# An attention and feed-forward kernel whose opening is reordered: batch 0 in overlapped halves, v used where it was loaded, batch 1 ahead of the output weights, one output tile held back

## The chip, the cores and the metric

The kernel runs on one core of a Trainium2 chip. The metric is device time in microseconds, from launch to end of one execution. A core has five engines that run side by side, each with its own instruction stream in order: PE (TensorE, matmuls), DVE (VectorE), ACT (ScalarE), POOL (GpSimd) and SP (SyncE, here only a DMA queue). They meet through semaphores. SBUF is the on-chip memory, PSUM the small memory into which PE writes its sums.

## What is computed

Eight batches of eight heads, 576 positions, head size 64: linear attention with an RMS norm, then a feed-forward layer over all 4608 tokens.

```python
kv = np.einsum('bhsd,bhse->bhde', k, v)
out = np.einsum('bhsd,bhde->bhse', q, kv)
rms = np.sqrt(np.mean(out * out, axis=-1, keepdims=True) + 1e-06)
attn = out / rms * g_norm
x = attn.transpose(0, 2, 1, 3).reshape(B * S, H * D)      # 4608 x 512
h = x @ w_in                                              # 512 x 2048
g = np.maximum(h, 0.0) + alpha * np.minimum(h, 0.0)
y = g @ w_out                                             # 2048 x 512
```

All inputs and the output are float32. The kernel computes in float16 with float32 sums.

## The kernel before, in words

The 4608 tokens are cut into nine windows of 512 tokens; a window does not end where a batch of 576 ends. Heads are taken in four pairs j, so that a pair fills 128 partitions.

**Loading.** All loads are issued from POOL, in program order, and are cast to float16 on the way. The first 512 positions of a batch go to a staging tile (`kst`, `vst`, `qst`, two of each), whose partition p holds positions 4p to 4p+3 of every head; the last 64 positions, the remainder, go straight to the fifth slot of the batch's tile (`ksb`, `vsb`, `qsb`, three of each). Regrouping (`regroup`, L133) copies staging to the batch's tile, so that the two heads of a pair lie side by side.

**Attention of a pair.** `step_t` transposes q by five matmuls of 128 columns and evacuates on DVE (qt). `step_kv` sums k times v over five matmuls; DVE masks the result (kv). `step_ot` multiplies them into a tile of 512 tokens (ot), which ACT squares. `step_ssq` sums the squares by a matmul with a block mask; ACT takes Ln and Exp (`rstd`), and DVE writes the normalised tile `xt`. qt and kv share one PSUM buffer (`ps_s`), ot has two, ssq has one.

**Feed-forward.** For window w and each of 16 groups g of 128 hidden units: four w_in matmuls (`m1_mm`) into one of three `h` buffers, evacuated by ACT (`m_sb`) and DVE (`gt`). Then a tile a of 128 tokens gets 16 w_out matmuls (`y_mm`), one for each g; ACT copies it (`y_out`) and SP stores it.

**Order.** The program is recorded in the order in which it is written, engine by engine. Opening: batch 0 in two halves of four heads, one after the other; ten matmuls on constants at the start, and a few between (`keep_warm`), only keep PE busy. First pass over w_in: 16 groups of window 0. First pass over w_out: the four tiles ya, yb, yc, yd of window 0 at once (three of them in the h buffers), g outermost, with window 1's attention steps put in from g = 6. Loop of window 1: its w_in groups, with window 2's attention from g = 4. From window 2 on a loop holds w_in of w, w_out of w - 1 and attention of w + 1. The last window's w_out follows alone.

**Queues around the change.** POOL issues batch 0, the four quarters of w_in, then batch 1 and w_out mixed, then batches 2 and 3. Regrouping stands on DVE (and for v of batch 0 on ACT) up to batch 2, on POOL from batch 3 on.

## Time and profile before

| | |
|---|---|
| median of three runs | 329.71 us (329.23 to 330.53) |
| profiled execution | 329.75 us, span 328.0 us |
| PE busy | 298.4 us, 91% |
| ACT, DVE, POOL busy | 53%, 49%, 23% |
| mean granted clock of PE | 0.99 |
| w_in matmul of 512 columns, mean | 384 ns x576 |
| w_out matmul of 512 columns, mean | 379 ns x512 |

The means are longer than the pace, since matmuls follow each other before the one ahead has left the array. A row of the timeline gives start, duration and, in brackets, how long the engine stood idle before it and what ended that. A row of waits gives who waited for whom, the sum, the number and the longest. In the table of stages the three numbers at the end are granted clock, mean number of busy DMA slots per engine and GB/s.

### The profile page before, as it was taken

Reading aid. Unit: us, or ns where it says so; the run is one execution under the profiler, and the core shown is the slowest. Engines: PE = TensorE matmul, PEld = TensorE weight load, DVE = VectorE, ACT = ScalarE, POOL = GpSimd, SP = SyncE. Lnnn points to the kernel's source line nnn. Section 1 sums busy time; section 2 is a strip of 40 time slices with the busy share of each in tenths; the row PEclk is TensorE's granted clock in tenths of the full one; section 3 lists DMA queues with packets and bytes.
Section 4 is the critical chain, followed back from the end, with each engine's and each line's share of the span. In section 5 each row is a group of like instructions: output and inputs, shape, how many; then the busy total and the mean of one; then the engine's idle time right before and its main releaser. Section 6 shows DMA issues by size and latency. Waiting matters only on the chain.

```text
span 328.0 us, 4205 instructions
## 1 busy us (share of the span) xinstructions
PE 298.4 (91%) x1593; PEld 143.7 (44%) x1593; DVE 160.2 (49%) x271; ACT 173.4 (53%) x291; POOL 74.7 (23%) x80
## 2 busy tenths in 40 slices
...
GB/s 95 193 203 202 198 195 191 223 145 83 38 178 33 34 126 154 34 33 149 134 32 34 32 32 34 51 13 53 36 23 21 59 38 34 32 32 34 44 86 64
DMA packets 47621, 28.07 MB, mean 86 GB/s; under 512 B 14304, under 2 KB 42992, under 8 KB 47600
## 3 DMA queue, kind: packets, MB, share of 16 engines
...
## 4 chain that ended last, share of the span: by engine, by line
PE 83%; ACT 7%; DVE 4%; DMA 2%; issue 1%; POOL 1%; POOLq 0%; ACTq 0%
PE h_ps L300 36%; PE y_ps L322 34%; PE kv_ps L237 3%; PE ssq_ps L268 2%; PE qt_ps L222 2%; PE ot_ps L256 2%; ACT rstd L270 2%; DMA qsb<-in_q_dram 2%; ACT rstd L273 2%; DVE xt L275 1%; DVE gt L309 1%; ACT sq_sb L262 1%; ACT m_sb L307 1%; PE yd L322 1%; DVE qt_sb L231 1%
## 5 line engine op out<-in xcount | busy, mean ns | idle before, releaser
L300 PE MATMUL h_ps<-xt,w_in_sb 128*128 128x512 f16 x576 | 147.3, 384 | 4.1 <-ACT y_sb L329 1.5
L309 DVE SCALAR_TENSOR_TENSOR gt<-m_sb,beta_sb,h_ps 128x512 f16<-128x512 f32 x144 | 106.8, 745 | 88.4 <-ACT m_sb L307 86.9
L307 ACT ACTIVATE m_sb<-h_ps 128x512 f32<-128x512 f32 x144 | 85.1, 593 | 83.7 <-PE h_ps L300 83.6
L322 PE MATMUL y_ps<-w_out_sb,gt 128*128 128x512 f16 x512 | 128.8, 379 | 0.0
L322 PEld LDWEIGHTS <-gt 128*128 128x128 f16 x576 | 56.0, 98 | 67.5 <-issue 2.3
L300 PEld LDWEIGHTS <-w_in_sb 128*128 128x128 f16 x576 | 54.9, 99 | 67.2 <-issue 14.5
L275 DVE SCALAR_TENSOR_TENSOR xt<-ot_ps,g2col,rstd 128x512 f16<-128x512 f32 x36 | 27.0, 751 | 46.5 <-ACT rstd L273 46.5
L270 ACT ACTIVATE rstd<-ssq_ps,eps_t 128x512 f32<-128x512 f32 x36 | 24.7, 686 | 18.2 <-PE ssq_ps L268 18.2
L262 ACT ACTIVATE sq_sb<-ot_ps 128x512 f16<-128x512 f32 x36 | 21.3, 597 | 22.6 <-PE ot_ps L256 22.1
L329 ACT COPY y_sb<-y_ps 128x512 f32<-128x512 f32 x32 | 18.7, 585 | 18.4 <-PE y_ps L322 18.4
L273 ACT ACTIVATE rstd<-rstd 128x512 f32<-128x512 f32 x36 | 22.7, 629 | 1.1
L268 PE MATMUL ssq_ps<-sq_sb,mask 128*128 128x512 f16 x36 | 13.6, 378 | 7.0 <-ACT sq_sb L262 5.5
L222 PE MATMUL qt_ps<-ident,qsb 128*128 128x128 f16 x160 | 14.8, 227 | 5.7 <-DVE qsb L139 4.8
L237 PE MATMUL kv_ps<-vsb,ksb 128*128 128x128 f16 x160 | 14.5, 226 | 4.7 <-DVE qt_sb L231 4.7
L222 PEld LDWEIGHTS <-qsb 128*128 128x128 f16 x160 | 11.8, 101 | 13.5 <-DVE qsb L139 5.9
L231 DVE COPY qt_sb<-qt_ps 128x576 f16<-128x576 f16 x32 | 14.3, 451 | 6.4 <-PE qt_ps L222 6.3
L237 PEld LDWEIGHTS <-ksb 128*128 128x128 f16 x160 | 11.9, 101 | 12.1 <-issue 6.1
L256 PE MATMUL ot_ps<-qt_sb,kv_sb 128*128 128x512 f16 (+7 forms) x64 | 14.2, 296 | 0.3 <-DVE kv_sb L245 0.3
L128 POOL DMA_DIRECT2D ksb<-in_k_dram x8 | 5.6, 700 | 36.4 <-PE kv_ps L237 27.8
L139 POOL COPY ksb<-kst 128x2048 f16<-128x2048 f16 x5 | 9.5, 1893 | 18.7 <-DMA kst<-in_k_dram 18.7
L139 POOL COPY qsb<-qst 128x2048 f16<-128x2048 f16 x5 | 9.5, 1894 | 7.4 <-DMA qst<-in_q_dram 7.4
L139 POOL COPY vsb<-vst 128x2048 f16<-128x2048 f16 x5 | 9.5, 1894 | 6.8 <-DMA vst<-in_v_dram 6.8
...
## 6 DMA issues: line engine op xcount, KB each, us to landing
...
```

What stands on the lines that cost most here:

```text
L139: (eng or nc.vector).tensor_copy(out=dst, in_=src)
L222: nc.tensor.matmul(out=qt_ps[:, t * P : (t + 1) * P], lhsT=qs[:, t, 2 * j : 2 * j + 2, :], rhs=ident16[:], is_transpose=True, start=(t == ...
L237: nc.tensor.matmul(out=kv_ps[:], lhsT=ks[:, t, 2 * j : 2 * j + 2, :], rhs=vs[:, t, 2 * j : 2 * j + 2, :], start=(t == 0), stop=(t == NT - 1),)
L256: nc.tensor.matmul(out=ot_ps[:, n0 - w * W : n1 - w * W], lhsT=kvs[b, j][:], rhs=qts[b, j][:, n0 - b * S : n1 - b * S], start=True, stop=True,
L262: nc.scalar.activation(out=sq[:], in_=ot_ps[:], func=AF.Square)
L270: nc.scalar.activation(out=rstd[:], in_=ssq_ps[:], func=AF.Ln, bias=eps_t[:], scale=inv_d,)
L273: nc.scalar.activation(out=rstd[:], in_=rstd[:], func=AF.Exp, bias=0.0, scale=-0.5)
L275: nc.vector.scalar_tensor_tensor(out=xts[w, j][:], in0=ot_ps[:], scalar=g2col[:], in1=rstd[:], op0=ALU.mult, op1=ALU.mult,)
L300: nc.tensor.matmul(out=h_ps[:], lhsT=w_in_blk(c, g), rhs=xts[w, c][:], start=(c == 0), stop=(c == NC - 1),)
L307: nc.scalar.activation(out=m_sb[:], in_=h_ps[:], func=AF.Relu, scale=-1.0)
L309: nc.vector.scalar_tensor_tensor(out=gt[:], in0=m_sb[:], scalar=beta_sb[:, g : g + 1], in1=h_ps[:], op0=ALU.mult, op1=ALU.add,)
L322: nc.tensor.matmul(out=y[:], lhsT=gts[w, g][:, a * P : (a + 1) * P], rhs=w_out_blk(g), start=(g == 0), stop=(g == NF - 1),)
```

## The change

- The remainder of batch 0 is loaded by SP as float32 into three output buffers; ACT casts it into place.
- v is no longer regrouped. `step_kv` reads its four main slices from the staging tile as two runs of 64 columns that lie 256 elements apart, and the fifth from the small `vsb` tile.
- POOL loads batch 0 as q, k, v of heads 0 to 3, then of heads 4 to 7; k and q of batch 1 come ahead of the first quarter of w_out, v of batch 1 right behind it.
- In the opening the transposes and kv products of the second half stand before the end of the first half's normalisation (`ssq_mm` and `norm` are now apart).
- Batch 1's k and q are regrouped on DVE inside the first pass over w_in, batch 2's on POOL.
- The first pass over w_out makes three tiles, with window 1's attention spread from g = 0 to g = 12; the fourth tile's 16 matmuls go into window 1's loop, one for each g.

```diff
@@ -94,6 +94,12 @@
     warm16 = const_p.tile([P, W], FP16, name="warm16")
     nc.vector.memset(warm16[:], 0.5)
 
+    rem0 = {}
+    for nm, src in (("q", q), ("k", k), ("v", v)):
+        rem0[nm] = ysb_p.tile([P, H, D], FP32, name=f"rem0{nm}", tag="y_sb")
+        nc.sync.dma_start(
+            out=rem0[nm][0:REM], in_=src[0, :, MAIN:S, :].rearrange("h s d -> s h d"),
+        )
     alpha_row = const_p.tile([NF, P], FP32, name="alpha_row")
     nc.sync.dma_start(out=alpha_row[:], in_=moe_alpha[:].rearrange("(g p) -> g p", p=P))
     g2col = const_p.tile([P, 1], FP32, name="g2col")
@@ -109,8 +115,9 @@
     for i in range(NBUF):
         t = {}
         for nm in ("k", "v", "q"):
-            t[nm] = qkv_p.tile([P, NT, H, D], FP16, name=f"{nm}sb{i}")
-            nc.vector.memset(t[nm][REM:P, TPP, :, :], 0.0)
+            n = 1 if nm == "v" else NT
+            t[nm] = qkv_p.tile([P, n, H, D], FP16, name=f"{nm}sb{i}")
+            nc.vector.memset(t[nm][REM:P, n - 1, :, :], 0.0)
         bufs.append(t)
     stages = {}
 
@@ -126,7 +133,7 @@
 
     def load_rem(b, nm):
         nc.gpsimd.dma_start(
-            out=bufs[b % NBUF][nm][0:REM, TPP, :, :],
+            out=bufs[b % NBUF][nm][0:REM, 0 if nm == "v" else TPP, :, :],
             in_=srcs[nm][b, :, MAIN:S, :].rearrange("h s d -> s h d"),
         )
 
@@ -144,7 +151,7 @@
             load_main(b, nm, 0, H)
 
     def regroup_batch(b):
-        for nm in ("k", "v", "q"):
+        for nm in ("k", "q"):
             regroup(b, nm, 0, H, nc.gpsimd)
 
 
@@ -178,25 +185,21 @@
         i, r = divmod(g, GW)
         return w_out_sb[i][:, r, :]
 
-    for nm in ("k", "v", "q"):
-        load_main(0, nm, 0, H // 2)
-    for nm in ("k", "v", "q"):
-        load_rem(0, nm)
-    for nm in ("k", "v", "q"):
-        load_main(0, nm, H // 2, H)
+    for h0 in (0, H // 2):
+        for nm in ("q", "k", "v"):
+            load_main(0, nm, h0, h0 + H // 2)
     for i in range(WQ):
         load_w_in(i)
-    load_batch(1, ("k",))
+    load_batch(1, ("k", "q"))
     load_w_out(0)
-    load_w_out(1)
-    load_batch(1, ("v", "q"))
-    load_w_out(2)
-    load_w_out(3)
+    load_batch(1, ("v",))
+    for i in range(1, WQ):
+        load_w_out(i)
     load_batch(2)
 
 
     def keep_warm(n):
-        ps = ps_y.tile([P, W], FP32, name="warm_ps", tag="y")
+        ps = ps_s.tile([P, W], FP32, name="warm_ps", tag="s")
         for i in range(n):
             nc.tensor.matmul(out=ps[:], lhsT=mask16[:], rhs=warm16[:], start=True, stop=True)
 
@@ -215,13 +218,22 @@
 
     qts, kvs, xts = {}, {}, {}
 
+    def pair_cols(b, nm, j):
+        def f(t):
+            if nm == "v" and t < TPP:
+                return stages[b, nm][:, 2 * j : 2 * j + 2, t, :]
+            if nm == "v":
+                return bufs[b % NBUF][nm][:, 0, 2 * j : 2 * j + 2, :]
+            return bufs[b % NBUF][nm][:, t, 2 * j : 2 * j + 2, :]
+        return f
+
     def step_t(b, j, pool=(ps_s, "s")):
-        qs = bufs[b % NBUF]["q"]
+        qs = pair_cols(b, "q", j)
         qt_ps = pool[0].tile([P, NT * P], FP16, name="qt_ps", tag=pool[1])
         for t in range(NT):
             nc.tensor.matmul(
                 out=qt_ps[:, t * P : (t + 1) * P],
-                lhsT=qs[:, t, 2 * j : 2 * j + 2, :],
+                lhsT=qs(t),
                 rhs=ident16[:],
                 is_transpose=True,
                 start=(t == 0),
@@ -231,13 +243,13 @@
         nc.vector.tensor_copy(out=qts[b, j][:], in_=qt_ps[:, 0:S])
 
     def step_kv(b, j, pool=(ps_s, "s")):
-        ks, vs = bufs[b % NBUF]["k"], bufs[b % NBUF]["v"]
+        ks, vs = pair_cols(b, "k", j), pair_cols(b, "v", j)
         kv_ps = pool[0].tile([P, P], FP32, name="kv_ps", tag=pool[1])
         for t in range(NT):
             nc.tensor.matmul(
                 out=kv_ps[:],
-                lhsT=ks[:, t, 2 * j : 2 * j + 2, :],
-                rhs=vs[:, t, 2 * j : 2 * j + 2, :],
+                lhsT=ks(t),
+                rhs=vs(t),
                 start=(t == 0),
                 stop=(t == NT - 1),
             )
@@ -247,8 +259,11 @@
 
     ots = {}
 
-    def step_ot(w, j):
-        ot_ps = ps_o.tile([P, W], FP32, name="ot_ps", tag="o")
+    def step_ot(w, j, pool=None):
+        if pool is not None:
+            ot_ps = pool[0].tile([P, W], FP32, name="ot_ps", tag=pool[1])
+        else:
+            ot_ps = ps_o.tile([P, W], FP32, name="ot_ps", tag="o")
         n0 = w * W
         while n0 < (w + 1) * W:
             b = n0 // S
@@ -263,6 +278,10 @@
         ots[w, j] = (ot_ps, sq)
 
     def step_ssq(w, j):
+        ssq_mm(w, j)
+        norm(w, j)
+
+    def ssq_mm(w, j):
         ot_ps, sq = ots.pop((w, j))
         ssq_ps = ps_q.tile([P, W], FP32, name="ssq_ps", tag="q")
         nc.tensor.matmul(out=ssq_ps[:], lhsT=mask16[:], rhs=sq[:], start=True, stop=True)
@@ -271,6 +290,10 @@
             out=rstd[:], in_=ssq_ps[:], func=AF.Ln, bias=eps_t[:], scale=inv_d,
         )
         nc.scalar.activation(out=rstd[:], in_=rstd[:], func=AF.Exp, bias=0.0, scale=-0.5)
+        ots[w, j] = (ot_ps, rstd)
+
+    def norm(w, j):
+        ot_ps, rstd = ots.pop((w, j))
         xts[w, j] = xt_p.tile([P, W], FP16, name="xt", tag=f"xt{j}")
         nc.vector.scalar_tensor_tensor(
             out=xts[w, j][:], in0=ot_ps[:], scalar=g2col[:], in1=rstd[:],
@@ -343,26 +366,34 @@
 
 
     H_POOL = (ps_h, "h")
-    for j0 in (0, 2):
-        regroup(0, "q", 2 * j0, 2 * j0 + 4)
-        regroup(0, "v", 2 * j0, 2 * j0 + 4, nc.scalar)
-        regroup(0, "k", 2 * j0, 2 * j0 + 4)
-        j1 = j0 + 1
-        step_t(0, j0, H_POOL)
-        step_t(0, j1, H_POOL)
-        step_kv(0, j0)
-        step_kv(0, j1, H_POOL)
-        step_ot(0, j0)
-        step_ot(0, j1)
-        if j0 == 0:
-            keep_warm(4)
-            step_ssq(0, j0)
-            step_ssq(0, j1)
-            keep_warm(6)
+    for nm in ("q", "k", "v"):
+        nc.scalar.copy(out=bufs[0][nm][0:REM, 0 if nm == "v" else TPP, :, :], in_=rem0[nm][0:REM])
+    regroup(0, "q", 0, H // 2)
+    step_t(0, 0, H_POOL)
+    regroup(0, "k", 0, H // 2)
+    step_t(0, 1, H_POOL)
+    keep_warm(3)
+    step_kv(0, 0)
+    step_kv(0, 1, H_POOL)
+    step_ot(0, 0)
+    step_ot(0, 1)
+    regroup(0, "q", H // 2, H)
+    step_t(0, 2, H_POOL)
+    regroup(0, "k", H // 2, H)
+    step_t(0, 3, H_POOL)
+    ssq_mm(0, 0)
+    ssq_mm(0, 1)
+    norm(0, 0)
+    step_kv(0, 2)
+    step_kv(0, 3, H_POOL)
+    norm(0, 1)
+    step_ot(0, 2)
+    step_ot(0, 3, (ps_y, "y"))
     first = [ps_h.tile([P, W], FP32, name="h_ps", tag="h") for g in range(3)]
     for g in range(3):
         m1_mm(first[g], 0, g, (0, 1))
     step_ssq(0, 2)
+    keep_warm(2)
     step_ssq(0, 3)
     for g in range(3):
         m1_mm(first[g], 0, g, (2,))
@@ -371,26 +402,28 @@
         m1_evac(first[g], 0, g)
     for g in range(3, NF):
         m1_group(0, g)
-
-
-    for nm in ("q", "k", "v"):
-        regroup(1, nm, 0, H)
+        if g == 10:
+            regroup(1, "k", 0, H)
+        if g == 14:
+            regroup(1, "q", 0, H)
+
+
+    AHEAD = 3
     ys = [
         ps_y.tile([P, W], FP32, name="ya", tag="y"),
         ps_h.tile([P, W], FP32, name="yb", tag="h"),
         ps_h.tile([P, W], FP32, name="yc", tag="h"),
-        ps_h.tile([P, W], FP32, name="yd", tag="h"),
     ]
     steps = window_steps(1)
+    n = len(steps)
     for g in range(NF):
-        for a in range(TPW):
+        for a in range(AHEAD):
             y_mm(ys[a], 0, a, g)
-            if g >= 6 and steps and (a == 1 or (a == 3 and g >= 8)):
+            if a != 1 and steps and n - len(steps) < n * (AHEAD * g + a + 1) // (AHEAD * (NF - 3)):
                 steps.pop(0)()
-    for a in range(TPW):
+    for a in range(AHEAD):
         y_out(ys[a], 0, a)
-    for f in steps:
-        f()
+    regroup_batch(2)
 
     for w in range(1, NW):
         steps = window_steps(w + 1) if w + 1 < NW else []
@@ -402,12 +435,16 @@
         y = None
         for g in range(NF):
             if w == 1 and g == first_g - 1:
-                for nm in ("q", "k", "v"):
-                    regroup(2, nm, 0, H)
                 load_batch(3)
                 regroup_batch(3)
             m1_group(w, g)
-            if w > 1:
+            if w == 1:
+                if g == 0:
+                    y = ps_y.tile([P, W], FP32, name="y_ps", tag="y")
+                y_mm(y, 0, AHEAD, g)
+                if g == NF - 1:
+                    y_out(y, 0, AHEAD)
+            else:
                 a, part = divmod(g, TPW)
                 if part == 0:
                     y = ps_y.tile([P, W], FP32, name="y_ps", tag="y")
```

The order in which POOL issues loads, from the last quarter of w_in on. Before (`kst`, `vst`, `qst` are the main parts, `ksb`, `vsb`, `qsb` the remainders):

```order
L159 DMA w_in_sb_155<-in_moe_w_in_dram 128x4x512
L128 DMA ksb_125<-in_k_dram 64x8x64
L122 DMA kst<-in_k_dram 128x8x256
L167 DMA w_out_sb_160<-in_moe_w_out_dram 128x4x512
L167 DMA w_out_sb_162<-in_moe_w_out_dram 128x4x512
L128 DMA vsb_127<-in_v_dram 64x8x64
L122 DMA vst<-in_v_dram 128x8x256
L128 DMA qsb_129<-in_q_dram 64x8x64
L122 DMA qst<-in_q_dram 128x8x256
L167 DMA w_out_sb_170<-in_moe_w_out_dram 128x4x512
L167 DMA w_out_sb_172<-in_moe_w_out_dram 128x4x512
```

Now:

```order
L166 DMA w_in_sb_158<-in_moe_w_in_dram 128x4x512
L135 DMA ksb_131<-in_k_dram 64x8x64
L129 DMA kst<-in_k_dram 128x8x256
L135 DMA qsb_135<-in_q_dram 64x8x64
L129 DMA qst<-in_q_dram 128x8x256
L174 DMA w_out_sb_166<-in_moe_w_out_dram 128x4x512
L135 DMA vsb_133<-in_v_dram 64x8x64
L129 DMA vst<-in_v_dram 128x8x256
L174 DMA w_out_sb_171<-in_moe_w_out_dram 128x4x512
L174 DMA w_out_sb_173<-in_moe_w_out_dram 128x4x512
L174 DMA w_out_sb_175<-in_moe_w_out_dram 128x4x512
```

q of batch 1 moved ahead of the first quarter of w_out, and v ahead of the second.

DVE in the opening, from the first regrouping of batch 0 to its last normalisation. Before:

```order
L139 COPY qsb_123<-qst 128x4x4x64
L139 COPY ksb_119<-kst 128x4x4x64
L231 COPY qt_sb<-qt_ps 128x576 x2
L245 TENSOR_TENSOR kv_sb<-kv_ps,mask_102 128x128 x2
L275 SCALAR_TENSOR_TENSOR xt<-ot_ps,g2col,rstd 128x512 x2
L139 COPY qsb_123<-qst 128x4x4x64
L139 COPY ksb_119<-kst 128x4x4x64
L231 COPY qt_sb<-qt_ps 128x576 x2
L245 TENSOR_TENSOR kv_sb<-kv_ps,mask_102 128x128 x2
```

Now, from the first kv on:

```order
L257 TENSOR_TENSOR kv_sb<-kv_ps,mask_102 128x128 x2
L146 COPY qsb_129<-qst 128x4x4x64
L243 COPY qt_sb<-qt_ps 128x576
L146 COPY ksb_125<-kst 128x4x4x64
L243 COPY qt_sb<-qt_ps 128x576
L298 SCALAR_TENSOR_TENSOR xt<-ot_ps,g2col,rstd 128x512
L257 TENSOR_TENSOR kv_sb<-kv_ps,mask_102 128x128 x2
L298 SCALAR_TENSOR_TENSOR xt<-ot_ps,g2col,rstd 128x512 x3
```

The two normalisations (`xt`) that stood ahead of the second half's regrouping now stand behind it.

DVE at the end of the first pass over w_in (`gt` is the evacuation of a group). Before:

```order
L309 SCALAR_TENSOR_TENSOR gt<-m_sb,beta_sb,h_ps 128x512 x16
L139 COPY qsb_129<-qst 128x8x4x64
L139 COPY ksb_125<-kst 128x8x4x64
L139 COPY vsb_127<-vst 128x8x4x64
L231 COPY qt_sb<-qt_ps 128x576
```

Now:

```order
L332 SCALAR_TENSOR_TENSOR gt<-m_sb,beta_sb,h_ps 128x512 x11
L146 COPY ksb_131<-kst 128x8x4x64
L332 SCALAR_TENSOR_TENSOR gt<-m_sb,beta_sb,h_ps 128x512 x4
L146 COPY qsb_135<-qst 128x8x4x64
L332 SCALAR_TENSOR_TENSOR gt<-m_sb,beta_sb,h_ps 128x512
L243 COPY qt_sb<-qt_ps 128x576
```

Batch 1's regrouping moved in between the evacuations, and v's is gone.

## The prediction

> **What bounds the kernel now.** I read the page first, then a table of five stages, then who waited for whom in each of the first four.
>
> ```profile
> span 328.0 us, 4205 instructions
> PE 298.4 (91%) x1593; PEld 143.7 (44%) x1593; DVE 160.2 (49%) x271; ACT 173.4 (53%) x291; POOL 74.7 (23%) x80
> ```
>
> ```profile
> core 0: us, PE busy (x) PEld busy (x) DVE busy (x) ACT busy (x) POOL busy (x), PEclk, DMA share, GB/s
> 0.00:27.87 27.87, 16.77 (x82) 7.69 (x82) 11.81 (x35) 11.95 (x18) 17.37 (x28) 1.00 1.22 168
> 27.87:39.09 11.22, 11.22 (x52) 5.08 (x52) 9.52 (x14) 7.31 (x13) 4.57 (x6) 1.00 1.43 198
> 39.09:62.46 23.37, 18.75 (x117) 9.37 (x116) 9.08 (x17) 9.15 (x16) 9.34 (x9) 0.99 1.49 190
> 62.46:90.91 28.45, 22.83 (x120) 10.81 (x120) 17.95 (x30) 16.92 (x30) 17.02 (x16) 0.88 0.80 115
> 90.91:328.00 237.09, 228.88 (x1225) 110.77 (x1223) 111.80 (x178) 128.03 (x216) 26.44 (x21) 1.00 0.31 57
> ```
>
> PE carries the kernel. After 90.91 it is busy 228.88 of 237.09 us and the change leaves its instructions there alone, so I put that stage at zero. The loss lies in the first 91 us: the opening, the first pass over w_in (call it A, 27.87 to 39.09, full), the first pass over w_out with window 1's attention in it (B, 39.09 to 62.46) and the loop of window 1 (C, 62.46 to 90.91). DMA moves about 200 GB/s without a break until 62 us, so arrival times are the second limit.
>
> Waits of PE in B, then waits of all engines in C:
>
> ```profile
> PE kv_ps L237 <- DVE qt_sb L231: 1.6, 2, 0.8
> PE h_ps L300 <- ACT y_sb L329: 1.5, 1, 1.5
> PE ssq_ps L268 <- ACT sq_sb L262: 0.8, 1, 0.8
> ```
> ```profile
> PE kv_ps L237 <- DVE qt_sb L231: 3.1, 3, 1.9
> PE ssq_ps L268 <- ACT sq_sb L262: 1.2, 1, 1.2
> PEld L222 <- DVE qsb L139: 1.1, 1, 1.1
> PE qt_ps L222 <- DVE kv_sb L245: 0.7, 2, 0.4
> ```
>
> C has a second loss, the clock. Four short stretches, PE alone:
>
> ```profile
> 58.90:62.30 3.40, 1.24 (x5) 0.98 1.37 173
> 62.30:65.70 3.40, 3.24 (x8) 0.52 0.90 288
> 68.90:72.30 3.40, 1.32 (x9) 1.00 1.47 172
> 72.30:75.70 3.40, 3.01 (x16) 0.52 1.57 191
> ```
>
> Each stretch with PE busy under 1.4 of 3.4 us is followed by one at about half clock. That costs (3.24 + 3.01) x 0.48 = 3.0 us.
>
> **The change part by part.** The unit prices come from the timeline of PE: 52 matmuls of 512 columns in 11.38 us, the last carrying 0.38, so 11.0 / 51 = 0.216 us each; ten of 128 columns in 0.73, so 0.28 us for five.
>
> ```profile
> 18.88 0.73 PE L222 MATMUL qt_ps<-ident,qsb 128*128 128x128 f16 x10 [1.35 <-DVE qsb L139]
> 20.89 1.46 PE L300 MATMUL h_ps<-xt,w_in_sb 128*128 128x512 f16 x6
> 26.03 0.81 PE L300 MATMUL h_ps<-xt,w_in_sb 128*128 128x512 f16 x3 [0.43 <-DVE xt L275]
> 27.87 11.38 PE L300 MATMUL h_ps<-xt,w_in_sb 128*128 128x512 f16 x52 [1.03 <-DVE gt L309]
> ```
>
> *Opening.* Today the second half of batch 0 is regrouped only after the first half's normalisation (PE waits 1.35 us at 18.88), although it had landed at 14.90. After the change the transposes and products of heads 4 to 7 run before the first two normalisations. What then limits the first six w_in matmuls is the arrival of w_in and of the last v. POOL's row of DMA issues dates them: an issue that waits for a transfer starts when that transfer has landed.
>
> ```profile
> 14.90 0.74 POOL L167 DMA_DIRECT2D w_out_sb<-in_moe_w_out_dram  x1 [0.59 <-DMA qst<-in_q_dram]
> 17.43 0.70 POOL L128 DMA_DIRECT2D vsb<-in_v_dram  x1 [1.79 <-DMA w_in_sb<-in_moe_w_in_dram]
> 25.14 0.88 POOL L122 DMA_DIRECT2D qst<-in_q_dram  x1 [1.93 <-DMA w_in_sb<-in_moe_w_in_dram]
> 28.14 0.74 POOL L167 DMA_DIRECT2D w_out_sb<-in_moe_w_out_dram  x1 [1.38 <-DMA kst<-in_k_dram]
> 30.70 0.69 POOL L128 DMA_DIRECT2D ksb<-in_k_dram  x1 [1.82 <-DMA w_out_sb<-in_moe_w_out_dram]
> 39.50 0.88 POOL L122 DMA_DIRECT2D qst<-in_q_dram  x1 [0.72 <-DMA qst<-in_q_dram]
> 44.85 0.88 POOL L122 DMA_DIRECT2D kst<-in_k_dram  x1 [1.93 <-DMA w_out_sb<-in_moe_w_out_dram]
> ```
>
> Batch 0's last half lands at about 14.9, the first w_in at 17.43. From the last v: two kv groups (0.73), their evacuation (about 0.5) and two ot (0.6) end at 16.7, ahead of w_in. The three remainder pieces leave POOL's queue for SP's, which can start before POOL's first transfer; they still take the DMA engines, as float32. I allow 0.2 us earlier: six matmuls at 17.2 instead of 20.89, **-3.7**. What follows (two ssq, Ln, Exp, xt, the last c) keeps its order, so the 6.98 us to the full rate stay. Bounds: -2.0 (one normalisation and its evacuations still in the way; or one 3.4 us stretch at half clock) and -4.6 (w_in 0.9 us earlier). The Trainium skill (Trainium Kernel Development and Optimization, Key Constraints) says that DMAs of the SP and POOL queues share the same 16 engines and interleave, so the SP queue gives no extra bandwidth. By it alone the term would be -3.5; the 198 GB/s of the table, the same in each full stretch, agrees.
>
> *A.* Regrouping batch 1's k and q moves in here on DVE, 0.69 us each at the unhindered rate, between evacuations of about 0.7 us per 0.86 us of PE. With three h buffers the delay of 0.69 is made good in about four groups.
>
> ```profile
> 40.59 0.69 DVE L139 COPY qsb<-qst 128x2048 f16<-128x2048 f16 x1
> 68.07 0.93 DVE L139 COPY qsb<-qst 128x2048 f16<-128x2048 f16 x1
> 56.71 1.89 POOL L139 COPY ksb<-kst 128x2048 f16<-128x2048 f16 x1 [5.07 <-DMA kst<-in_k_dram]
> ```
>
> I book **+0.3** (0 to 1.4, both in full). Are they loaded? k 1 keeps its place at 28.1. A tensor with its remainder takes 28.14 - 25.14 = 3.0 us, so q 1 lands at about 31.1; a quarter of w_out takes 30.70 - 28.14 = 2.6. Group 10 is evacuated at about 24.2 + 8 x 0.86 = 31, group 14 at 34.5. DVE would hold all later evacuations if k were late; the margin is 3 us.
>
> *B.* Now starts at 39.1 - 3.4 = 35.7. Work: 48 instead of 64 y matmuls, 48 x 0.216 = 10.4, plus eight groups of five (2.2), plus four ot and four ssq (1.7): 14.3. Stalls go by two chains that the timeline shows: from one ssq to the kv behind it (Ln, Exp, xt, the next qt evacuation), and from one ssq to the last.
>
> ```profile
> 50.04 0.38 PE L268 MATMUL ssq_ps<-sq_sb,mask 128*128 128x512 f16 x1
> 53.01 0.44 PE L237 MATMUL kv_ps<-vsb,ksb 128*128 128x128 f16 x5 [0.80 <-DVE qt_sb L231]
> 57.39 0.38 PE L268 MATMUL ssq_ps<-sq_sb,mask 128*128 128x512 f16 x1
> 59.69 0.38 PE L268 MATMUL ssq_ps<-sq_sb,mask 128*128 128x512 f16 x1 [0.84 <-ACT sq_sb L262]
> 62.46 6.01 PE L300 MATMUL h_ps<-xt,w_in_sb 128*128 128x512 f16 x20 [1.53 <-ACT y_sb L329]
> ```
>
> 2.97 us from ssq to kv: in the new order PE has 7 y, one t, one ot and the ssq there (2.2), then 8 y (2.4): stalls 0.75 and 0.55. 2.30 us from ssq 2 to ssq 3, filled by five matmuls: 1.2. The 1.53 before window 1 goes: nine y stand behind ssq 3 (2.0 us, before only four), and the third h buffer is free because the fourth y tile no longer takes it. So 14.3 + 2.5 + 0.2 for the first y's evacuations = 17.0.
>
> Arrivals: up to w_out 1 the same transfers stand in the queue as before up to q 1, so w_out 1 comes at 39.5, and by the steps of 2.6 and 3.0 us v 1 at 36.9, w_out 0 at 33.9, w_out 2 at 42.2, w_out 3 at 44.8. B needs them at about 37, 35.7, 39.2, 43.5 and 48: a wait of about 0.4 at most for w_out 1. 17.4 against 23.37: **-6.0**. Bounds: -7 (no arrival or stall beyond one chain) and -3 (w_out 1 and v 1 each 1.5 us later).
>
> *C.* Now starts at 53.1. Before: 68 h matmuls (14.7), 2.2 and 1.7 = 18.6 of work; 28.45 - 18.6 = 9.85 lost, 3.0 by clock, the rest waits with about 0.16 us of drain at each. The 16 y matmuls of the held tile come in here, +3.45, 22.05 in all. DVE no longer regroups batch 2 here (the 1.9 us wait at kv and the 1.1 us at the first transpose stood behind it); POOL does it, 1.89 us a tensor. Batch 2's q lands at about 53, so POOL is done at 55; its first transpose stands at about 53.1 + 5 x 1.08 = 58.5. Cover 3 us. The other stalls (0.55, 0.64, 0.3, 0.4, 1.2 and their drains, 3.9) I keep, although each gets one y matmul more as cover; bounds 2.5 to 5. The clock: B's and C's worst 3.4 us hold at most 1.4 us of stall, so PE is busy 2.0, above the 1.3 that preceded each drop; I take no drop. 22.05 + 3.9 = 25.95 against 28.45: **-2.5** (-4 to +0.6). The Trainium skill (TensorE: Matmul & The Clock Gate, Part 1) has half clock after one idle window of about 3.4 us and none in between. The 0.52 agrees, but here a window 36% busy was enough; by the page's "idle" no drop would be expected either, so the sum is the same.
>
> *Free edits.* v used from its staging tile: POOL saves 1.89 us per batch off the path; its kv matmuls now read two runs of 64 columns. The row for contiguous v is 0.057 us each; nothing here shows a split operand. I take no cost, being nearest to the ot matmuls that start at column offsets; the far end is a rival.
>
> Sum: -3.7 + 0.3 - 6.0 - 2.5 = -11.9. The profiled execution took 329.75 us (span 328.0 and 1.75 around it), 0.04 from the median: **317.9 us**.
>
> **The rivals.**
>
> 1. *Arrivals bind in B* (14%). B's start moves up by 3.4 us and w_out 1 not at all (39.5). If the transfers lag by 2 us, or B's first groups run ahead, kv 0, group 4 and group 8 each wait: 2 to 4 us back, **321**. For it: 198 GB/s already unbroken. Against: margins of 1 to 4 us except at w_out 1.
> 2. *The clock still drops* (10%). Two stretches, 3.0 us: **321**. For it: before, 1.5 us of wait was enough. Against: more y work in each stretch.
> 3. *Stalls in C vanish* (6%): 3.9 us less, **314**. For it: one more y per group; against: the chains go through ACT and DVE behind h evacuations.
> 4. *Slower: split v reads* (4%). 4 of every 5 kv matmuls, 128 in all, read v at a step. If PE passed over the skipped columns too, each would cost what 512 columns cost, 0.216 instead of 0.057: 128 x 0.159 = 20 us, **338**. It decides from 0.09 us extra each (11.9 / 128). Against: runs of 64 columns are long. The Trainium skill (SBUF — State Buffer, Door 1, the note on cachelines) has full rate where accesses fall into the same 16-byte line and a penalty for sparser ones, which speaks for no cost; no run here shows it.
> 5. *The gain is lost later* (4%). load_batch(3) now stands behind POOL's regrouping of batch 2, 55 instead of 42 us. If batch 3 missed window 2's first transpose at about 79, the loop would start as late as before: **329**. Against: six issues of 0.9 and 9 us of transfer end, with regrouping, near 70.
>
> **How the numbers follow.** Forecast 62%. Within 0.5% (1.65 us), what a measurement of this kernel can hardly tell from no change: rival 5, 4%. Slower: rival 4, 4%. Faster: 62 + 14 + 10 + 6 = 92%. Adding the terms' bounds in full gives 312 to 329; they hardly fall together, so 312.5 to 324 reaches past rivals 1 to 3 and leaves out some 2 in 10.
>
> **What would show it.** Right: the first w_in matmuls at 17 to 18 us and the full rate near 24; w_out matmuls from about 35.7; window 1's first matmul near 53; window 2's first y matmul near 79; granted clock 1.0 throughout; the last 237 us unchanged. Wrong: POOL's w_out transfers named as releasers of PE in B (rival 1), a 5 or 7 in the clock row (2), kv groups over 0.44 us (4), a wait for qsb in window 2 (5). An opening that keeps its 20.89 would cost the forecast 3.7 us by itself.

## The result and the profile after

The changed kernel takes **319.38 us** (median of four runs, 318.95 to 319.83) against 329.47 us for the kernel before (328.71 to 330.53): a ratio of 0.9692, with a 95% interval of 0.966 to 0.9724. The forecast was 317.9 us. The profiled execution took 319.12 us, its span is 317.4 us. All ratios below leave out executions that took over 1.5% longer than the fastest of the same kernel; among the runs shown only one kernel, v in place alone, has such, three of its ten.

The table of stages of the changed kernel, cut at the same four events as before: the full rate of w_in, the first w_out matmul, window 1's first matmul, window 2's first y matmul.

```profile
0.00:25.46 25.46, 14.84 (x77) 6.99 (x78) 12.01 (x35) 11.69 (x19) 13.74 (x23) 0.93 1.14 166
25.46:36.98 11.52, 11.38 (x53) 5.05 (x53) 9.86 (x15) 7.30 (x13) 5.37 (x7) 1.00 1.47 197
36.98:54.61 17.63, 15.22 (x102) 7.73 (x100) 7.31 (x15) 8.38 (x14) 3.46 (x3) 1.00 1.34 184
54.61:80.46 25.85, 23.09 (x137) 11.48 (x136) 16.73 (x29) 17.98 (x33) 15.69 (x16) 1.00 1.00 135
80.46:317.40 236.94, 228.87 (x1224) 110.78 (x1223) 111.33 (x177) 128.07 (x216) 28.33 (x26) 1.00 0.36 63
```

The second number of a row is the stage's length. Against the terms of the prediction:

| stage | before | forecast change | measured change |
|---|---|---|---|
| opening | 27.87 | -3.7 | -2.41 |
| A, first pass over w_in | 11.22 | +0.3 | +0.30 |
| B, first pass over w_out | 23.37 | -6.0 | -5.74 |
| C, loop of window 1 | 28.45 | -2.5 | -2.60 |
| the rest | 237.09 | 0 | -0.15 |
| sum | | -11.9 | -10.6 |

Four of the five terms are met within 0.3 us. What is missing, 1.3 us, is missing in the opening, and the granted clock of that row, 0.93, is the only one below 1.00. PE's timeline there (start, duration, and in brackets the idle time ahead and what ended it):

```profile
8.94 0.20 PE L208 MATMUL alpha_ps<-ident,alpha_row 16*128 16x16 f32 x1 [2.58 <-DMA alpha_row<-in_moe_alpha_dram]
9.75 1.25 PE L234 MATMUL qt_ps<-ident,qsb 128*128 128x128 f16 x10 [0.60 <-DVE qsb L146]
12.33 0.51 PE L249 MATMUL kv_ps<-vst,ksb 128*128 128x128 f16 x4
18.70 1.24 PE L323 MATMUL h_ps<-xt,w_in_sb 128*128 128x512 f16 x5 [0.22 <-DVE xt L298]
```

Two things stand here that the forecast did not have. PE is idle for 2.58 us, because the small `alpha_row` that the program transposes ahead of everything else is late. And ten transposes then take 1.25 us, where the ten of the second half, at 14.29 us, take 0.73: PE runs at half clock from there to about 12.6. The half clock is not new. In the kernel before, the first ten transposes followed a pause of 2.89 us and took more than twice what its second ten took (0.73 us at 18.88), although its clock column reads 1.00 there:

```profile
9.87 1.57 PE L222 MATMUL qt_ps<-ident,qsb 128*128 128x128 f16 x10 [2.89 <-DVE qsb L139]
```

So both openings ran at half clock for a while, and the forecast, whose table had 1.00 for the opening before, priced it in neither. The first w_in matmuls came at 18.10 (one) and 18.70 (five) and not at 17.2; the full rate at 25.46 and not at 24.2.

In B the waits are the forecast ones. PE's two largest waits of B, then the rows of its three longest pauses and the first row of window 1:

```profile
PE ssq_ps L287 <- ACT sq_sb L277: 1.1, 1, 1.1
PE kv_ps L249 <- DVE qt_sb L243: 0.9, 2, 0.6
```

```profile
45.34 0.38 PE L249 MATMUL kv_ps<-vst,ksb 128*128 128x128 f16 x4 [0.58 <-DVE qt_sb L243]
49.23 0.38 PE L249 MATMUL kv_ps<-vst,ksb 128*128 128x128 f16 x4 [0.36 <-DVE qt_sb L243]
52.45 0.38 PE L287 MATMUL ssq_ps<-sq_sb,mask 128*128 128x512 f16 x1 [1.06 <-ACT sq_sb L277]
54.61 1.03 PE L323 MATMUL h_ps<-xt,w_in_sb 128*128 128x512 f16 x4
```

Forecast were 0.75, 0.55 and 1.2, and no wait ahead of window 1. No transfer ends a wait of PE in B. C's waits are 0.26, 0.75, 0.55 and 1.11 us, where 0.55, 0.64, 0.3, 0.4 and 1.2 were kept.

### The profile page after: what moved, and what is told of

Read it like the earlier page. It is cut to its first block, busy times and chain, and to the rows that moved or that the text cites. A ratio compares the mean times of both kernels' runs of the same rounds, so it can differ in the third digit from the quotient of the medians.

```text
span 317.4 us, 4195 instructions
## 1 busy us (share of the span) xinstructions
PE 293.4 (92%) x1588; PEld 142.0 (45%) x1588; DVE 157.2 (50%) x267; ACT 173.4 (55%) x292; POOL 66.6 (21%) x74
## 4 chain that ended last, share of the span: by engine, by line
PE 85%; ACT 6%; DVE 4%; DMA 2%; issue 1%; SPq 1%; ACTq 0%
PE h_ps L323 37%; PE y_ps L345 36%; PE qt_ps L234 3%; PE kv_ps L249 3%; PE ssq_ps L287 3%; PE ot_ps L271 2%; DMA alpha_row<-in_moe_alpha_dram 2%; ACT rstd L289 2%; ACT sq_sb L277 1%; ACT rstd L292 1%; DVE gt L332 1%; DVE xt L298 1%; ACT m_sb L330 1%; SPq L100 1%; PE yb L345 1%
## 5 line engine op out<-in xcount | busy, mean ns | idle before, releaser
L345 PE MATMUL y_ps<-w_out_sb,gt 128*128 128x512 f16 x528 | 134.8, 379 | 0.1
L323 PEld LDWEIGHTS <-w_in_sb 128*128 128x128 f16 x576 | 54.2, 98 | 64.2 <-issue 10.4
L277 ACT ACTIVATE sq_sb<-ot_ps 128x512 f16<-128x512 f32 x36 | 21.3, 596 | 16.2 <-PE ot_ps L271 15.6
L287 PE MATMUL ssq_ps<-sq_sb,mask 128*128 128x512 f16 x36 | 13.6, 378 | 6.7 <-ACT sq_sb L277 5.6
L129 POOL DMA_DIRECT2D vst<-in_v_dram x9 | 7.7, 860 | 50.4 <-PE kv_ps L249 48.6
L146 POOL COPY qsb<-qst 128x2048 f16<-128x2048 f16 x6 | 11.4, 1897 | 32.5 <-DMA qst<-in_q_dram 32.5
L271 PE MATMUL ot_ps<-qt_sb,kv_sb 128*128 128x512 f16 (+7 forms) x64 | 13.5, 286 | 0.8 <-DVE kv_sb L257 0.7
L249 PE MATMUL kv_ps<-vst,ksb 128*128 128x128 f16 x128 | 12.3, 220 | 1.8 <-DVE qt_sb L243 1.8
L146 POOL COPY ksb<-kst 128x2048 f16<-128x2048 f16 x6 | 11.4, 1903 | 11.9 <-DMA kst<-in_k_dram 11.9
L257 DVE TENSOR_TENSOR kv_sb<-kv_ps,mask 128x128 f16<-128x128 f32 x32 | 9.0, 285 | 3.8 <-PE kv_ps L249 3.8
```

The source lines that it names most:

```text
L146: (eng or nc.vector).tensor_copy(out=dst, in_=src)
L249: nc.tensor.matmul(out=kv_ps[:], lhsT=ks(t), rhs=vs(t), start=(t == 0), stop=(t == NT - 1),)
L277: nc.scalar.activation(out=sq[:], in_=ot_ps[:], func=AF.Square)
L287: nc.tensor.matmul(out=ssq_ps[:], lhsT=mask16[:], rhs=sq[:], start=True, stop=True)
L323: nc.tensor.matmul(out=h_ps[:], lhsT=w_in_blk(c, g), rhs=xts[w, c][:], start=(c == 0), stop=(c == NC - 1),)
L345: nc.tensor.matmul(out=y[:], lhsT=gts[w, g][:, a * P : (a + 1) * P], rhs=w_out_blk(g), start=(g == 0), stop=(g == NF - 1),)
```

## The experiments

Each was run beside the kernel before, whose median on those chips lay between 329.5 and 329.7 us. Two questions led them: what the 1.3 us in the opening are, and whether B and C were won by what the prediction named.

### The late alpha

`alpha_row` is issued on SP behind the three new float32 remainders. The view of DMA issues gives microseconds from issue to landing as the last number; first of the kernel before, then three of the changed one:

```profile
alpha_row<-in_moe_alpha_dram SPq DMA_DIRECT2D x1, 8.0 KB, 1.6
```

```profile
rem0q<-in_q_dram SPq DMA_DIRECT2D x1, 128.0 KB, 2.8
rem0v<-in_v_dram SPq DMA_DIRECT2D x1, 128.0 KB, 5.8
alpha_row<-in_moe_alpha_dram SPq DMA_DIRECT2D x1, 8.0 KB, 5.9
```

The obvious cure is to issue the small loads (`alpha_row` and the two of `g2col`) first.

```diff
+    alpha_row = const_p.tile([NF, P], FP32, name="alpha_row")
+    nc.sync.dma_start(out=alpha_row[:], in_=moe_alpha[:].rearrange("(g p) -> g p", p=P))
...
     rem0 = {}
     for nm, src in (("q", q), ("k", k), ("v", v)):
...
-    alpha_row = const_p.tile([NF, P], FP32, name="alpha_row")
-    nc.sync.dma_start(out=alpha_row[:], in_=moe_alpha[:].rearrange("(g p) -> g p", p=P))
...
```

> The changed kernel with one edit: alpha_row and the two g2col loads go out on SP ahead of the three float32 remainders. In the changed kernel alpha_row was issued behind the remainders, landed at 8.8 us, and PE (2.58 us idle, then half clock to 12.7) and DVE (beta_sb ahead of the first regrouping) stood behind it. Theory T1 (the shortfall of 1.2 us in the opening is this wait): PE reaches the first transposes about 1 us earlier, no half clock, the first w_in matmuls at about 17.4 and the full rate at about 24.3: total 1.0 to 1.2 us below the changed kernel, near 318.3. Theory T2 (the opening is limited by w_in and the last v, which land 0.85 us later than before because the remainders go as float32 through the same DMA engines): the wait at alpha goes, but the first w_in matmuls stay at 18.1 or later: gain 0 to 0.5, near 319.

Measured: 322.55 us (322.1 to 322.81), ratio 0.9789 (0.9761 to 0.9817), some 3 us slower than the changed kernel. DMA issues, then PE's timeline:

```profile
rem0q<-in_q_dram SPq DMA_DIRECT2D x1, 128.0 KB, 6.7
rem0v<-in_v_dram SPq DMA_DIRECT2D x1, 128.0 KB, 9.7
alpha_row<-in_moe_alpha_dram SPq DMA_DIRECT2D x1, 8.0 KB, 1.7
```

```profile
9.82 0.82 PE L234 MATMUL qt_ps<-ident,qsb 128*128 128x128 f16 x6 [2.20 <-ACT qsb L370]
14.23 0.27 PE L249 MATMUL kv_ps<-vsb,ksb 128*128 128x128 f16 x1 [1.67 <-ACT vsb L370]
20.80 2.43 PE L323 MATMUL h_ps<-xt,w_in_sb 128*128 128x512 f16 x6
```

alpha is there after 1.7 us. The remainders, issued 1.7 us later, pay for it: q takes 6.7 us instead of 2.8 and v 9.7 instead of 5.8, and PE waits for them twice; its half clock then lasts into the w_in matmuls, six in 2.43 us. Neither theory held: the wait at alpha went, and another came. Each of these loads is wanted at about the same time, so those issued later are waited for. That the later ones are slower because POOL's large transfers are by then under way is likely, but no run separates it.

The second attempt moved no load. The alpha matmul and the DVE instruction behind it (`beta_sb`) were put behind the first half's ot.

```diff
-    alpha_ps = ps_s.tile([P, NF], FP32, name="alpha_ps", tag="s")
-    nc.tensor.matmul(
-        out=alpha_ps[:], lhsT=alpha_row[:], rhs=ident[0:NF, 0:NF], is_transpose=True,
...
     step_ot(0, 0)
     step_ot(0, 1)
+    alpha_ps = ps_s.tile([P, NF], FP32, name="alpha_ps", tag="s")
+    nc.tensor.matmul(
+        out=alpha_ps[:], lhsT=alpha_row[:], rhs=ident[0:NF, 0:NF], is_transpose=True,
...
```

> The changed kernel with no load moved: only the alpha matmul on PE and beta_sb on DVE stand later, behind the two ot products of the first half. The wait of 2.58 us for alpha_row goes, and the order on every DMA queue stays. With the small loads first, the remainders had landed late (the cast of v's at 13.9) and PE waited for them; here they keep their place. Theory T1 (the alpha wait holds up the opening): the transposes run at about 7, the first kv at about 11.8 (v of the first half lands at 11.7) instead of 12.33, all later steps 0.5 us earlier where nothing else binds; the first w_in lands at about 18.1, so the first w_in matmuls hardly move and the full rate comes at 24.9 instead of 25.46: total 0.3 to 0.6 us below the changed kernel. Theory T2 (arrivals and the Ln/Exp chain bind, the alpha wait was covered): within 0.3 us. A longer pause ahead of the first kv may also cost a stretch of half clock, at most 1 us back.

Measured: 321.12 us (320.1 to 322.5), ratio 0.9743 (0.9714 to 0.9772): no gain, but 1.1 to 1.7 us more than the changed kernel's two medians (319.38 and, below, 320.00). PE's timeline, of the slowest of the six executions:

```profile
8.00 0.73 PE L225 MATMUL qt_ps<-ident,qsb 128*128 128x128 f16 x10 [1.69 <-DVE qsb L146]
11.83 0.38 PE L240 MATMUL kv_ps<-vst,ksb 128*128 128x128 f16 x4 [2.45 <-DMA vst<-in_v_dram]
14.51 1.25 PE L225 MATMUL qt_ps<-ident,qsb 128*128 128x128 f16 x10 [0.60 <-DVE qsb L146]
19.43 2.77 PE L314 MATMUL h_ps<-xt,w_in_sb 128*128 128x512 f16 x6
```

The transposes come 1.75 us earlier, and then kv waits for v, which lands no earlier, and comes only 0.5 us earlier (11.83 for 12.33). So **alpha's wait was hardly on the path**; the arrival of v was behind it. The pause is now ahead of kv, and the half clock follows this pause instead: ten transposes in 1.25 us at 14.51, and six w_in matmuls in 2.77 us instead of 1.46. There it does lie on the path. The theory that the wait for alpha cost the missing time falls.

With eight instead of three matmuls on constants in that gap:

```diff
-    keep_warm(3)
+    keep_warm(8)
```

> The same with eight instead of three matmuls on constants between the transposes and the first kv, which fills the pause up to the landing of v. If a stretch of half clock in the opening costs time on the path, this is 0.3 to 1 us faster than the alpha matmul late by itself; if arrivals bind, the same within 0.3 us.

320.09 us (319.97 to 320.33), ratio 0.9709 (0.9683 to 0.9736): the kv wait shrinks to 0.76 us, the half clock still comes (from about 13.6 to 20.5), and the time is that of the changed kernel. It is 1.0 us less than with the alpha matmul late by itself, the most that was expected; since a stretch of half clock is still there, this run does not say what the 1.0 us were.

The remainders on POOL's queue instead of SP's, in float16 as the program had them before:

```diff
     for nm in ("q", "k", "v"):
         load_main(0, nm, h0, h0 + H // 2)
+    if h0 == 0:
+        for nm in ("q", "k", "v"):
+            load_rem(0, nm)
```

> The changed kernel with the remainders of batch 0 back on POOL, cast to float16 on the way, behind the first halves; no casts on ACT; alpha_row alone at the head of SP's queue. T1: the same as with the small loads first, about 1.0 us below the changed kernel, since the wait at alpha is gone in both. T2: the first w_in lands at about 17.4 again instead of 18.2, so this is faster than the small loads first by up to 0.8 us. Against both: the first kv then waits for remainders that stand behind three half tensors, at about 11.5, so the first half may start no earlier than now (12.3) and the gain is 0 to 0.5.

319.66 us (319.5 to 320.01), ratio 0.9704 (0.9674 to 0.9734): the same as the changed kernel. alpha is early (6.16), and in its stead the transposes wait 2.51 us for the remainder of q. Taking the remainders off POOL's queue is thus worth nothing that these runs can tell. In this profile w_in did land 0.8 us earlier than in the changed kernel's (17.49 for 18.28 us by the POOL issue that waits for it), as the second theory had it, and nothing was won by it: the first w_in matmuls stand at 18.52 and 19.12, and the second of these waits for xt.

### What the half clock cost

Sixteen instead of ten matmuls on constants at the very start, and the same kernel unchanged beside it:

```diff
-    keep_warm(10)
+    keep_warm(16)
```

> The changed kernel with 16 instead of 10 matmuls on constants at the start, so that PE is busy until alpha lands at about 8.9 us. Theory (the stretch at half clock from 9.4 to 12.6 follows the idle 2.6 us ahead of the alpha matmul, and delays the first kv): full clock up to 12, first kv at about 11.8 instead of 12.3, 318.9 us. Rival (the half clock comes anyway after the next pause, at 12 to 16, as where the alpha matmul stood late): first w_in matmuls at 18.5 or later, 320 to 321 us.

> The changed kernel once more, on the chip of the runs beside it: 319.4 us, within 0.4. If the places of the half clock differ between executions, its profile shows them elsewhere than 9.4 to 12.6 us, with the same time within 1 us.

Sixteen: 319.96 us (318.12 to 321.04), ratio 0.9707 (0.9668 to 0.9746). Unchanged: 320.00 us (318.8 to 320.79), ratio 0.9716 (0.9682 to 0.9751). As kernels they are the same. But the profiled execution with sixteen is one that had no half clock anywhere, and so shows what the opening is without it:

```profile
9.26 0.20 PE L208 MATMUL alpha_ps<-ident,alpha_row 16*128 16x16 f32 x1 [1.39 <-DMA alpha_row<-in_moe_alpha_dram]
10.07 0.73 PE L234 MATMUL qt_ps<-ident,qsb 128*128 128x128 f16 x10 [0.60 <-DVE qsb L146]
11.50 0.38 PE L249 MATMUL kv_ps<-vst,ksb 128*128 128x128 f16 x4
17.57 1.47 PE L323 MATMUL h_ps<-xt,w_in_sb 128*128 128x512 f16 x6 [0.66 <-DMA w_in_sb<-in_moe_w_in_dram]
24.57 11.68 PE L323 MATMUL h_ps<-xt,w_in_sb 128*128 128x512 f16 x52 [1.04 <-DVE gt L332]
```

Here the six w_in matmuls wait for the arrival of w_in, as the prediction had it, and run at 17.57 (forecast 17.2); the full rate comes at 24.57 (24.2). Stage C ends at 79.56, the rest is 236.84 us, and the execution took 318.24 us, 0.3 us from the forecast. So of the 1.3 us missed, 0.89 us (25.46 - 24.57) lie between these two traces, and a w_in that came 0.4 us later than assumed, with no half clock about, is the rest.

The 0.89 us are not all clock. The POOL issue that waits for w_in dates its landing, first in the changed kernel's profile, then in that with sixteen:

```profile
18.28 0.75 POOL L174 DMA_DIRECT2D w_out_sb<-in_moe_w_out_dram  x1 [1.66 <-DMA w_in_sb<-in_moe_w_in_dram]
```

```profile
17.81 0.75 POOL L174 DMA_DIRECT2D w_out_sb<-in_moe_w_out_dram  x1 [1.62 <-DMA w_in_sb<-in_moe_w_in_dram]
```

In the first, w_in itself was 0.47 us later. But in the second profile of the unchanged kernel it was earlier than in either (17.50), the half clock stood at the same place (ten transposes in 1.25 us at 9.80; between these two executions it did not move), and yet the first w_in matmul came at 18.34, the next five at 18.93:

```profile
18.93 1.24 PE L323 MATMUL h_ps<-xt,w_in_sb 128*128 128x512 f16 x5 [0.22 <-DVE xt L298]
25.69 11.68 PE L323 MATMUL h_ps<-xt,w_in_sb 128*128 128x512 f16 x52 [1.04 <-DVE gt L332]
```

There the five wait for xt and not for w_in, and the full rate is 1.1 us behind that with sixteen, although alpha came 0.3 us sooner (8.94 for 9.26). So the half clock on PE's own chain is enough to lose what was missed; in the first profile a late w_in hides part of it.

It is not settled what makes one execution keep its clock. Of six executions with sixteen matmuls, three had a mean clock of 0.998 or 1.00 and took 318.1 to 319.2 us, three had 0.986 to 0.988 and took 320.7 to 321.0. The theory holds for the first three and the rival for the others; filling the pause moves the odds at most. Of the fourteen profiles of this case, that of the kernel before included, thirteen show a stretch of half clock in the opening and only this one shows none. The mean clock sorts executions only in part: two of the unchanged kernel with 1.00 took 319.83 and 319.88 us, longer than those with 0.993 to 0.996 (318.8 to 319.38), since the column can miss a stretch (last section).

### Batch 1 ahead of the output weights

The changed kernel with the old order of POOL's loads (q of batch 1 behind two quarters of w_out):

```diff
-    load_batch(1, ("k", "q"))
+    load_batch(1, ("k",))
     load_w_out(0)
-    load_batch(1, ("v",))
-    for i in range(1, WQ):
-        load_w_out(i)
+    load_w_out(1)
+    load_batch(1, ("v", "q"))
+    load_w_out(2)
+    load_w_out(3)
```

> The changed kernel with batch 1 and w_out loaded in the order of before (k, w_out 0, w_out 1, v, q, w_out 2, w_out 3). q of batch 1 then lands at about 40.3 instead of 32 us. DVE has its regrouping between groups 14 and 15 and blocks there from about 37.6 to 40.3; the first transpose of window 1 stands behind the third w_out matmul. Theory (q ahead of w_out is what lets the attention start at g = 0): PE stalls 2.5 to 3 us at the start of the pass over w_out, total 2 to 3 us slower than the changed kernel, near 322. Rival (order of loads does not matter, as the pass has 2.9 us of stalls that absorb it): within 0.5 us.

> The changed kernel with the old order of POOL's loads, another execution. Theory (in an execution whose first pass over w_in runs at full clock, q of batch 1 is the last to land, at about 40 us, and DVE stands at its regrouping from about 37.6): PE waits 2.5 to 3 us at the first transpose of window 1, 323 us. Rival (the old order costs through something else): that wait stays below 1 us and the loss of some 3.5 us stands elsewhere.

First run: 323.23 us (321.53 to 324.0), ratio 0.9804 (0.9765 to 0.9844). Its profile did not show why: that execution ran A at half clock for a while (13.81 us instead of 11.52), so q was in time, and it was the shortest of its runs. The second run, 323.34 us (323.30 and 323.38, ratio 0.9818, 0.9766 to 0.987), shows it. DVE, then PE:

```profile
40.23 0.69 DVE L146 COPY qsb<-qst 128x2048 f16<-128x2048 f16 x1 [2.86 <-DMA qst<-in_q_dram]
```

```profile
40.98 0.45 PE L235 MATMUL qt_ps<-ident,qsb 128*128 128x128 f16 x5 [3.18 <-DVE qsb L146]
```

q lands at 40.2, DVE stands at its regrouping, and PE waits 3.18 us at the first transpose; then the clock is at half for a stretch, and B takes 22.17 us (36.66 to 58.83) instead of 17.63. That is 4.5 us in this B, and 3.3 to 3.9 us in the medians, which hang on the order of the loads alone. The theory's 2.5 to 3 us for the wait was a little short, the time was as the second expectation said.

### The held output tile

```diff
-    AHEAD = 3
+    AHEAD = 4
     ys = [
...
+        ps_h.tile([P, W], FP32, name="yd", tag="h"),
     ]
...
-            if w == 1:
...
-                y_mm(y, 0, AHEAD, g)
...
-            else:
+            if w > 1:
```

> The changed kernel without the held tile: four output tiles in the first pass over w_out, the fourth in the third h buffer, no y matmuls in window 1's loop; everything else stays. The forecast's steps: the pass gets 16 matmuls (+3.45) and the 1.5 us wait for the copy of a y tile before window 1 comes back, its kv stalls go (about -0.9); window 1's loop loses 3.45 of work, its stalls grow by 0.2 us each (five of them, +1.0): the whole 1.5 to 2 us slower than the changed kernel, near 321. If the pause before window 1 makes the clock drop once more, 1.5 more, near 322.5. Rival: holding the tile back is worth nothing by itself and the gain came from loads and regrouping alone: same as the changed kernel within 0.5.

320.31 us (319.95 to 322.56), ratio 0.9737 (0.9696 to 0.9778). Its rows of B and C:

```profile
39.47:60.24 20.77, 18.57 (x117) 9.37 (x116) 7.77 (x15) 9.27 (x16) 7.81 (x8) 1.00 1.03 133
60.24:83.91 23.67, 19.73 (x121) 9.87 (x121) 15.72 (x27) 16.92 (x30) 10.66 (x11) 1.00 1.09 153
```

Together 44.44 us against 17.63 + 25.85 = 43.48: the held tile is worth 0.96 us in these two traces, less than the 1.5 to 2 expected, and 0.3 to 0.9 us by the medians, which is hardly clear of their spread. It mostly moves 16 matmuls from one stage to the next.

### Who regroups batch 2

In the prediction, C gained because POOL takes over the regrouping of batch 2. Put back on DVE:

```diff
-    regroup_batch(2)
...
+                for nm in ("q", "k"):
+                    regroup(2, nm, 0, H)
```

> The changed kernel with batch 2's k and q regrouped on DVE in window 1's loop at g = 3, as before, instead of on POOL. Theory (POOL's regrouping removed the long kv wait and with it the half clock in window 1): two copies of 0.7 to 1.0 us stand ahead of the evacuations of g = 4 and of the first qt, the first kv waits 1.5 to 2 us, total 1 to 2 us slower, near 321; with a stretch of half clock 1.5 more. Rival (the held tile's matmuls cover it): within 0.5 us of the changed kernel, no half clock.

320.11 us (319.29 to 321.64), ratio 0.9714 (0.9677 to 0.9751). The row of C and its first two waits, then the same two waits in the changed kernel:

```profile
56.27:82.14 25.87, 23.09 (x137) 11.49 (x136) 17.66 (x31) 17.96 (x33) 10.32 (x9) 1.00 0.92 126
```

```profile
63.81 0.38 PE L249 MATMUL kv_ps<-vst,ksb 128*128 128x128 f16 x4 [0.62 <-DVE qt_sb L243]
64.66 0.44 PE L234 MATMUL qt_ps<-ident,qsb 128*128 128x128 f16 x5 [0.41 <-DVE kv_sb L257]
```

```profile
61.79 0.38 PE L249 MATMUL kv_ps<-vst,ksb 128*128 128x128 f16 x4 [0.26 <-DVE qt_sb L243]
62.98 0.44 PE L234 MATMUL qt_ps<-ident,qsb 128*128 128x128 f16 x5 [0.75 <-DVE kv_sb L257]
```

25.87 against 25.85 us. The kv wait is 0.62 instead of 0.26 and the next 0.41 instead of 0.75: the sums are the same (1.03 and 1.01 us). **That step of the prediction is wrong**: the regrouping on POOL gained nothing, although C came out within 0.1 us of the forecast.

### What won stage C

The new opening with v in place and all else as in the kernel before: old load order, four tiles, attention from g = 6 on, q and k of batches 1 and 2 regrouped on DVE where they were. Against the changed kernel (the edit of the loads is that under "Batch 1 ahead of the output weights"):

```diff
-        if g == 10:
-            regroup(1, "k", 0, H)
-        if g == 14:
-            regroup(1, "q", 0, H)
+    for nm in ("q", "k"):
+        regroup(1, nm, 0, H)
...
-    AHEAD = 3
+    AHEAD = 4
...
-            if a != 1 and steps and n - len(steps) < n * (AHEAD * g + a + 1) // (AHEAD * (NF - 3)):
+            if g >= 6 and steps and (a == 1 or (a == 3 and g >= 8)):
...
-    regroup_batch(2)
...
+                for nm in ("q", "k"):
+                    regroup(2, nm, 0, H)
```

> The new opening (batch 0 in overlapped halves, remainders on SP, v in place) with the rest as before: batch 1 and w_out in the old order, batch 1's k and q regrouped on DVE behind the first pass over w_in, four tiles with attention from g = 6, batch 2's k and q on DVE in window 1. Theory (the parts add): the gain of the opening, 2.4 us, is all that is left, 327.3. Rival (the gain of the opening is worth something only because the loads of batch 1 come earlier too: the pass over w_out starts before q 1, at 37 against 40.3, and waits): the regrouping of q blocks DVE but the first transpose stands at about 42, so nothing is lost at kv; up to 1 us back, 328.3.

322.94 us (322.64 to 323.89), ratio 0.9802 (0.9765 to 0.9839): 4.4 us better than expected. Its rows of B and C:

```profile
36.44:59.81 23.37, 18.74 (x117) 9.37 (x116) 8.56 (x16) 9.15 (x16) 9.13 (x10) 1.00 1.47 189
59.81:84.15 24.34, 19.91 (x120) 9.79 (x120) 16.66 (x29) 16.92 (x30) 8.44 (x8) 1.00 0.81 119
```

B is what it was before, to the last digit. C is 4.1 us shorter (28.45 to 24.34), with nothing gone from its order but the copies of v, on DVE for batch 2 and on POOL for batch 3. Then v in place alone, on the kernel before, with a full `vsb` replaced by its fifth slot and no copy of v on DVE, ACT or POOL:

```diff
-                rhs=vs[:, t, 2 * j : 2 * j + 2, :],
+                rhs=vs(t),
...
-                for nm in ("q", "k", "v"):
+                for nm in ("q", "k"):
                     regroup(2, nm, 0, H)
```

> The kernel before, with v used from its staging tile and no other edit. Theory (the clock of window 1's loop was lost through the three DVE copies of batch 2, so leaving one out is enough): the kv wait of 1.9 us in that loop falls to about 1.0, the granted clock there to 1.0, the loop takes about 24.5 us instead of 28.45, and the kernel about 326 us. Rival (the drop of the clock is set by where the earlier pauses fall, and needs the shifted opening): only the shorter copies count, about 1 us, and the kernel takes about 328.5 us.

328.21 us in the median of ten executions, which lie between 325.05 and 332.05; ratio 0.9928 (0.989 to 0.9966). The median is the rival's; the stage is the theory's. Opening, A and C:

```profile
0.00:28.48 28.48, 17.41 (x81) 7.87 (x82) 11.82 (x35) 9.97 (x16) 17.82 (x29) 0.83 1.22 168
28.48:41.62 13.14, 13.14 (x53) 5.59 (x53) 9.52 (x14) 7.31 (x13) 5.03 (x7) 0.85 1.41 200
64.99:89.34 24.35, 19.91 (x121) 9.79 (x120) 16.66 (x29) 16.93 (x30) 8.42 (x8) 1.00 0.80 118
```

C is 24.35 us at full clock, 4.1 less. In the trace the kv wait there fell from 1.93 to 0.96 us, the first transpose's from 0.59 to 0.35, and the 3.0 us of half clock are gone: together 4.2. What the median does not show was lost earlier: the opening took 0.6 us more than in the kernel before and A, partly at half clock (0.85), 1.9 us more. The edit changes nothing in A, and the pause of 1.07 us shortly ahead of it is the same in all fourteen profiles; in three others (old load order, four tiles, the alpha matmul late) A was also partly at half clock and took 13.81, 13.83 and 12.24 us, in the other ten 11.22 to 11.87. Its best executions, with a mean clock of 0.991 to 0.995, took 325.05 to 325.55 us.

Why the drop in C goes when v stays in place is only half shown. In the 3.4 us that end at the longest kv wait, PE is busy 2.08 us, which were 1.32 before. But the drop ahead of it, at window 1's start, went too, although the pause there did not change at all. The same 3.4 us in the kernel before, and in this one:

```profile
58.90:62.30 3.40, 1.24 (x5) 0.48 (x5) 1.50 (x2) 2.90 (x7) 1.89 (x1) 0.98 1.37 173
```

```profile
61.59:64.99 3.40, 1.24 (x5) 0.48 (x5) 1.50 (x2) 2.90 (x7) 2.63 (x2) 1.00 1.20 143
```

Both have five matmuls and 1.24 us of PE; before it was followed by a stretch at 0.52, here by 20 matmuls at full clock. In all thirteen profiles with v in place C has a clock of 1.00, but only in two of them, this one and that of the new opening with the rest as before, is the 1.53 us pause ahead of window 1 still there. Of the kernel before there is one trace, so how often it drops there is open; its 39 executions beside these runs have mean clocks of 0.97 to 0.990, while those with v in place reach 0.995 and more, which fits a drop that comes there each time but does not show it.

## Why the prediction was right, and where not

**Opening, -3.7 forecast, -2.41 measured.** Where the clock was full, in the one profile without a drop, the reordering did what was worked out: w_in set the first w_in matmuls, and the 6.98 us from there to the full rate stayed (24.57 - 17.57 = 7.00). The term was mis-sized at the step "I allow 0.2 us earlier: six matmuls at 17.2". By the POOL issue that had dated w_in at 17.43 it landed at 17.50 to 18.28 in three profiles, so not earlier. And two things were not priced: the queue on SP, past which `alpha_row` moved (1.6 us became 5.9), and the half clock after a pause in the opening. The wait itself cost 0.5 us at most, since v came behind it; the half clock cost up to 1.1 us where w_in was in time. It stood in the kernel before too (ten transposes in 1.57 us), where the prediction went by the clock column's 1.00; what the reordering is worth with full clock on both sides is therefore not shown. The bound of -2.0, written for "one 3.4 us stretch at half clock", was the right one to have.

**A, +0.3.** Right. k and q lie between the evacuations and cost 0.30 us; in the run that regroups them behind the pass A takes 11.22 us again.

**B, -6.0 forecast, -5.74 measured.** Right, with its parts: stalls of 0.58, 0.36 and 1.06 us for 0.75, 0.55 and 1.2, no wait ahead of window 1, and loads in time. The runs split it: with the old load order B takes 22.17 us, with four tiles 20.77 us, with both old and the attention from g = 6 it was 23.37 us. Spreading the attention over the pass was not undone by itself, so its own share is open.

**C, -2.5 forecast, -2.60 measured.** The size was right, a cause was wrong. "POOL does it" was booked as what takes the 1.9 us and 1.1 us waits away; on DVE they stay away as well (25.87 us). With v's copy gone DVE needs two copies of 0.69 us in place of three of 0.93, 1.05 and 0.67; with v in place alone the kv wait goes from 1.93 to 0.96 us and the first transpose's from 0.59 to 0.35. The prediction had filed v in place under "free edits" and counted only POOL's time for it. The 3.0 us of clock were forecast rightly, by a threshold (PE busy under 1.4 of 3.4 us) that does not hold: the same 1.24 us came with and without a drop. Even the trace from which it was taken speaks against it: from 22.57 to 25.97 us PE is busy 1.18 us, and the three w_in matmuls behind take 0.81 us, as at full clock.

**The rest, 0.** Right, -0.15 us; `load_batch(3)` behind POOL's regrouping delayed nothing.

**The rivals.** Arrivals binding in B: refuted, no transfer releases PE there. A clock that still drops: in the two profiles of the changed kernel it does, but in the opening and not in B and C. The stalls in C stayed, 3.8 us (25.85 less 22.05 of work). Split reads of v: refuted. The kv matmuls of the changed kernel:

```profile
16.23 0.38 PE L249 MATMUL kv_ps<-vst,ksb 128*128 128x128 f16 x4
16.45 0.22 PE L249 MATMUL kv_ps<-vsb,ksb 128*128 128x128 f16 x1
```

Four of them in 0.22 us are 0.055 us each, as for contiguous v. Batch 3 too late: refuted, no wait for `qsb` in window 2.

**The sum of the bounds.** The terms' bounds add up to -15.6 and -3.0 us, which is 314.2 to 326.8 us and not the "312 to 329" that the prediction gives; the range that it states, 312.5 to 324, reaches further down than that and holds the result.

The expectation that the parts add up was not in the prediction but in the experiments, and there it failed: the opening with v in place gave 6.7 us of some 10, because the clock of C came with it, and the loads, the spread attention and the held tile the other 2.9 to 3.6, by the changed kernel's two medians.
